# A hand-written order of 368 pieces replaced by another: memory-compressed attention followed by a maxout FFN on one core

## The chip, the cores and the metric

The kernel runs on one core of one Trainium2 chip. The metric is the device time of one execution in microseconds; lower is better. The kernel before takes 165.37 us (median of three runs, 165.14 to 165.49). TensorE is called PE, VectorE DVE, ScalarE ACT, GpSimd POOL and SyncE SP, as the profile does.

## The reference

Eight batches, eight heads, 576 positions, head size 64, 32 memory slots; then a feed-forward layer over 4608 rows of width 512 with a hidden width of 768.

```python
a = exp(phi - max(phi, axis=2)); a = a / sum(a, axis=2)       # softmax over positions
k_m = einsum('bhsm,bhsd->bhmd', a, k)                         # 32 slots instead of 576 keys
v_m = einsum('bhsm,bhsd->bhmd', a, v)
scores = q @ k_m.T / sqrt(64)
attn = softmax(scores)                                        # over the 32 slots
x = (attn @ v_m)  ->  rows (batch, position), columns (head, d)
h = maximum(maximum(x @ w1, x @ w2), x @ w3)
out = h @ w_out                                               # 4608 x 512, float32
```

## The kernel before, in words

All inputs are loaded with a cast to bf16 by POOL's DMA queue, except `phi`, which stays float32 (batch 0's `phi` comes through SP's queue). The 576 x 64 attention output is never formed. Because x = attn v_m, the kernel multiplies v_m into the weights for each batch ("fold") and applies the 32 slot weights to the folded weights. It also uses max(a, b, c) = max(a - c, b - c, 0) + c: w1 - w3 and w2 - w3 are formed in place, the relu of the first is a drain, the second is combined in a max, and the w3 part goes straight through `w3o` = w3 w_out into the output sum.

The work is cut into pieces, and one text, the word list at the end of the function, gives their order. A word is `letter+number@batch`; each piece issues its instructions on all engines at once, and every engine executes its own instructions strictly in the order of the list. So the list sets the order on PE, DVE, ACT, POOL and on the DMA queues. The letters, with the engine of the main work:

- `Y` weights, `L` and `H` inputs (k, v, q, phi; H loads half of the heads): DMA issues on POOL. `r`: POOL copies k or v into a packed tile (line 104).
- `E`: exp of phi on ACT (230). `B`: memory keys and values on PE (244). `N`: their normalisation on DVE (262 to 276). `K`: transposes of them on PE (291) and the drain of these (173 on ACT, 177 on DVE).
- `Q`: two transposes of q on DVE (306). `S`: scores on PE (326), then two exps on ACT (335). `a`, `s`, `c`: transpose, sum and reciprocal on DVE (380, 388, 397). `m`: slot softmax multiply on POOL (402). `X`: transpose back into `attn` on DVE (410). In batch 0 `M`, `R` and a DVE multiply (370) do this instead.
- `D0` to `D2`: folds of w1/w2 on PE (433) with a drain of 128x1024 from two PSUM banks into bf16 tile `wp`; `D3` the same for `w3o`. Batch 0 has `D4` too and shorter folds.
- `F0` to `F11`: first layer on PE (459). The even ones are drained with a relu (171 on ACT, 175 on DVE), the odd ones are combined with that on DVE by a max into `hT` (472).
- `T0` to `T4`: second layer on PE (490, 499, 508), drain into a float32 tile `ot` and a store on SP's queue. Odd batches have a fifth, `T4`, which spans two batches. The last, `T3@7`, is split in two (531 to 551).
- `W`, `O`: transposes of w3 and the product w3 w_out, once. `V`: the subtraction w - w3 on DVE (214). `Z`: matmuls on zeros at the start (160). `I`: constants.

PSUM has eight banks. Each piece takes the next digit of a second text, the bank list, as the number of its bank (a pair of banks for `B`, `S`, `D`, `F`, `M`; `S` takes two pairs). A bank's next piece waits until its drain is done.

Which engine drains a piece is read from a table, and a `!` behind a word exchanges ACT and DVE:

```python
EVAC = {"D": "avaaa", "T": "vavav", "K": "v", "W": "vvv", "O": "aaaa", "F": "aaaaaa"}
```

In the profile line 173 is ACT's copy (tiles `wp`, `ot`, `kvt`, `w3o`), line 177 DVE's, and matmul lines carry the tile `psum`.

Of the kernel before, what the change touches and what calls it, by code (L numbers as in the profile page):

```python
# [15 lines left out]
def kernel(  # L16
# [12 lines left out]
    nc = tc.nc  # L29

    B, H, S, D = q.shape
# [54 lines left out]
    def load_ph(b):  # L86
        ph = inp.tile([P, NP, NC, M], FP32, name="ph")
        loaded.setdefault(b, {})["ph"] = ph
        dst = ph.rearrange("p j c m -> p j (c m)")
        if b == 0:  # L90
            for h in halves:
                nc.sync.dma_start(out=dst[:, h], in_=by_pair(phi, b)[:, h])
        else:
            nc.gpsimd.dma_start(out=dst, in_=by_pair(phi, b))
# [8 lines left out]
    def pack(b, i):  # L103
        nc.gpsimd.tensor_copy(  # L104
            out=kvrs[b % 2][:, :, :, D * i : D * (i + 1)], in_=kvos[b % 2][:, i]
        )

    def load_q(b):
        qq = inp.tile([P, NP, NC, D], BF16, name="qq")
        loaded.setdefault(b, {})["q"] = qq  # L110
        nc.gpsimd.dma_start(  # L111
            out=qq.rearrange("p j c d -> p j (c d)"), in_=by_pair(q, b)
        )

    def load_w(i):
        w = (moe_w1, moe_w2, moe_w3)[i]
        nc.gpsimd.dma_start(
            out=w_sb[:, :, i], in_=w.rearrange("(j p) f -> p j f", p=P)
        )
# [3 lines left out]
    def load_wo():  # L123
        nc.gpsimd.dma_start(out=wo_sb, in_=moe_w_out.rearrange("(t p) c -> p t c", p=P))
# [8 lines left out]
    for i in range(P // M):  # L133
# [5 lines left out]
    banks = iter(  # L139
        "".join(  # L140
            """
            00224460026701101401264026402640264026452063420643064206420642064562074206742064
            20642064201640264102640264026402640264072406247026402640264024602406520462046204
            62704267402640264124602416420642064206420642067676767670
            """.split()
        )
    )
# [4 lines left out]
    def two_banks():  # L152
        i = int(next(banks))
        return psum[:, i : i + 2]
# [10 lines left out]
    EVAC = {"D": "avaaa", "T": "vavav", "K": "v", "W": "vvv", "O": "aaaa", "F": "aaaaaa"}  # L165

    def evacuate(kind, n, swap, out_, in_, relu=False):

        if (EVAC[kind][n] == "a") != swap:
            if relu:  # L170
                nc.scalar.activation(out=out_, in_=in_, func=AF.Relu)  # L171
            else:
                nc.scalar.copy(out=out_, in_=in_)  # L173
        elif relu:
            nc.vector.tensor_scalar_max(out=out_, in0=in_, scalar1=0.0)
        else:
            nc.vector.tensor_copy(out=out_, in_=in_)
# [28 lines left out]
    def columns(b, n):  # L206
        return FIRST[n] if b == 0 else (n * BANK, (n + 1) * BANK)
# [188 lines left out]
        s = st[b]  # L396
        nc.vector.reciprocal(out=s["sm", g], in_=s["sm", g])  # L397

    def att_mul(b, g):
        s = st[b]  # L400
        t = s["t", g]
        nc.gpsimd.tensor_tensor(  # L402
            out=t,
            in0=t,
            in1=s["sm", g].unsqueeze(2).to_broadcast([P, S // HP, R, 2]),
            op=ALU.mult,
        )
# [7 lines left out]
    wps, wp3s = {}, {}  # L415

    def fold(b, n, swap):

        s = st[b]
        lo, hi = (0, DM) if n == 3 else columns(b, n)  # L420
        if n == 3:
            wp3s[b] = quad.tile([P, NG, DM], BF16, name="wp3")
        elif b not in wps:
            wps[b] = work.tile([P, NG, 2 * DF], BF16, name="wp")
        ps = two_banks()
        terms = [(s["kvt"][:, 0], w3o[:, :, lo:hi] if n == 3 else w12[:, :, lo:hi])]
        if b == 0 and n != 3:
            terms.append((s["kvtn"], w_sb[:, :, 2, lo % DF : lo % DF + hi - lo]))
        for i, (lhs, rhs) in enumerate(terms):
            for j in range(NP):  # L430
                for a in range(NG):
                    r = slice(HP * a, HP * (a + 1))
                    nc.tensor.matmul(  # L433
                        ps[M * j : M * (j + 1), a, 0 : hi - lo],
                        lhsT=lhs[r, M * j : M * (j + 1)],
                        rhs=rhs[r, j, :],
                        start=(i == 0),
                        stop=(i == len(terms) - 1),
                        tile_position=(HP * a, M * j),
                    )  # L440
        evacuate(
            "D", n, swap, wp3s[b] if n == 3 else wps[b][:, :, lo:hi], ps[:, :, 0 : hi - lo]
        )


    hts = {}
# [107 lines left out]
    def issue(b, n, swap):  # L554

        i = int(n[1:]) if len(n) > 1 else None
        {
            "I": lambda: [make_identity(nc, ident)]
            + [nc.gpsimd.memset(x[:, :, :, 2 * D : 2 * D + 1], 1.0) for x in kvrs],
            "Y": lambda: load_w(i) if i < 3 else load_wo(),  # L560
            "L": lambda: load_ph(b) if i == 0 else load_q(b) if i == 3 else load_kv(b, i - 1),
            "H": lambda: load_kv(b, i % 2, halves[i // 2]),
            "r": lambda: pack(b, i),
            "E": lambda: [att_exp(b, h) for h in (halves if b == 0 else [slice(0, NP)])],
            "B": lambda: att_kv(b, i),
            "N": lambda: att_kv_norm(b, i),
            "K": lambda: att_kv_t(b, swap, i),
            "Q": lambda: att_q(b, i),
            "S": lambda: att_score(b),
            "a": lambda: att_t(b, i),  # L570
            "s": lambda: att_sum(b, i),
            "c": lambda: att_rec(b, i),
            "m": lambda: att_mul(b, i),
            "X": lambda: (ones_mul if (b, i) in ONES else att_back)(b, i),
            "M": lambda: ones_sum(b, i),
            "R": lambda: ones_rec(b, i),
            "D": lambda: fold(b, i, swap),
            "F": lambda: ffn1(b, i, swap),
            "T": lambda: ffn2(b, i, swap),
            "W": lambda: w3_t(i, swap),  # L580
            "O": lambda: w3_o(i, swap),
            "V": lambda: w_diff(i),
            "Z": lambda: warm_up(i),
        }[n[0]]()


    for w in """
        E@0 H2@0 H0@0 L3@0 Z25@0 B0@0 I@0 N0@0 Z2@0 K0@0! Q0@0 Q1@0 Z9@0 S@0 Z2@0 M0@0 M1@0
        R0@0 Y2@0 R1@0 W0@0 Y3@0 W1@0 W2@0 Z6@0 O1@0 H3@0 O3@0 O2@0 H1@0 X1@0 B1@0 X0@0 N1@0
        K1@0 O0@0 Y0@0 D1@0! D0@0! D3@0 F8@0 F10@0 F2@0 V0@0 F6@0 F0@0! Y1@0 D2@0 D4@0 F4@0  # L590
        L0@1 V1@0 F1@0 E@1 F3@0 L1@1 F5@0 F9@0 F7@0 L3@1 F11@0 B0@1 T3@0 N0@1 K0@1! L2@1 Q1@1
        L2@2 L1@2 Q0@1 L0@2 V2@0 T0@0! L3@2 S@1 T1@0 a0@1 s0@1 c0@1 m0@1 B1@1 N1@1 a1@1 L1@3
        K1@1 s1@1 D0@1 D1@1! D2@1 c1@1 m1@1 X0@1 L3@3 r1@2 X1@1 T2@0! L2@3 F6@1 F10@1 F7@1 F2@1
        F3@1 F4@1 F0@1 r0@2 E@2 F5@1 F1@1 F11@1 L0@3 L0@4 F8@1 L2@4 F9@1 B@2 D3@1 N@2 Q1@2
        T0@1! K@2 T2@1! r0@3 Q0@2 S@2 a0@2 a1@2 s1@2 c1@2 m1@2 T4@1! D1@2! s0@2 D2@2 c0@2 m0@2
        X1@2 D0@2 T3@1 Q0@3 L3@4 X0@2 Q1@3 T1@1 F0@2 F4@2 F8@2 F6@2 F9@2 E@3 F7@2 r1@3 F5@2
        F10@2 F1@2 B@3 L1@4 D3@2 N@3 L0@5 F2@2 F11@2 E@4 F3@2 L1@5 K@3 r1@4 L2@5 T2@2! S@3 T3@2
        a0@3 s0@3 c0@3 m0@3 D0@3 D2@3 a1@3 s1@3 c1@3 X0@3 D1@3! Q0@4 m1@3 T1@2 L3@5 L2@6 T0@2!
        X1@3 F10@3 r0@4 F2@3 F4@3 E@5 Q1@4 r0@5 F5@3 F3@3 L1@6 F8@3 B@4 N@4 D3@3 F9@3 F6@3
        F11@3 L0@6 K@4 F0@3 F7@3 F1@3 S@4 a0@4 T4@3! s0@4 a1@4 D0@4 c0@4 s1@4 r1@5 c1@4 D3@4  # L600
        m0@4 X0@4 Q0@5 T0@3! D1@4! D2@4 B@5 T3@3 m1@4 X1@4 L0@7 F10@4 Q1@5 N@5 F8@4 K@5 F6@4
        F9@4 S@5 F7@4 L3@6 F2@4 F4@4 a0@5 L1@7 a1@5 F0@4 s0@5 r1@6 F3@4 D0@5 r0@6 s1@5 c1@5 E@6
        D3@5 m1@5 c0@5 F1@4 T1@3 L2@7 F11@4 L3@7 E@7 F5@4 m0@5 B@6 D1@5! D2@5 X1@5 N@6 T2@3!
        X0@5 F6@5 F8@5 Q0@6 Q1@6 K@6 F4@5 F9@5 S@6 F7@5 r0@7 a0@6 F2@5 a1@6 s0@6 c0@6 F0@5
        F10@5 m0@6 F1@5 s1@6 c1@6 F11@5 F5@5 T0@4! F3@5 X0@6 T2@4! r1@7 D0@6 D1@6! Q0@7 B@7
        m1@6 N@7 X1@6 T2@5! K@7 T3@4 Q1@7 S@7 a0@7 F2@6 s0@7 a1@7 s1@7 c1@7 m1@7 c0@7 F4@6
        T4@5! D3@6 D2@7 D0@7! T0@5! D3@7 D2@6 X1@7 m0@7 D1@7! T1@4 X0@7 F6@7 F3@6 T1@5 F4@7
        F8@7 F0@7 F5@6 F10@6 F7@7 F9@7 F10@7 F5@7 F0@6 F11@7 F6@6 F1@7 F7@6 F2@7 F8@6 F11@6
        F9@6 F1@6 F3@7 T0@6! T0@7! T3@5 T2@7! T2@6! T1@6 T1@7 T3@6 T4@7! T3@7
    """.split():  # L610
        n, b = w.rstrip("!").split("@")
        issue(int(b), n, w.endswith("!"))


# [28 lines left out]
```

## Time and profile before

| | |
|---|---|
| median of three runs | 165.37 us |
| span of the profiled execution, first to last instruction | 163.1 us |
| the profiled execution's own time | no time of it is given beside its span; the median is 2.27 us longer than the span |
| PE busy | 152.5 us (93%), 2060 matmuls |
| ACT, DVE, POOL busy | 100.6, 94.3, 69.6 us |
| granted PE clock, mean | 0.997 |
| loaded and stored by DMA | 31.77 MB, mean 195 GB/s |

Line numbers (L459) are those of the kernel. In a group's row the count follows the x, then the busy time of the group and the mean length of one in ns. A matmul's length in a row includes the time in which it overlaps its neighbours; what one costs in a row of matmuls is read from the chain, where 48 in 5.88 us are 0.1225 us each. In the chain, each row is start, length, and the work that the end waited for.

### The profile page before, as it was taken

How to read it: one execution, taken by the hardware profiler on the slowest of the kernel's cores; microseconds unless marked ns; L12 is line 12 of the kernel's file. 1: busy time of each engine (PE TensorE's matmuls, PEld its weight loads, DVE VectorE, ACT ScalarE, POOL GpSimd, SP SyncE). 2: the span in 40 equal slices, each digit the busy share in tenths (PEclk: the TensorE clock that was granted, in tenths of full speed). 3: DMA queues.
4: the chain of work that ended last, by engine and by line, in shares of the span. 5: the costliest groups of instructions: out<-in, count | busy, mean ns of one | idle time of the engine just before them, and what ended most of it. 6: DMA issues, size and time to landing. Idle time of an engine off the chain costs nothing.

```text
span 163.1 us, 4818 instructions
## 1 busy us (share of the span) xinstructions
PE 152.5 (93%) x2060; PEld 85.2 (52%) x2080; DVE 94.3 (58%) x181; ACT 100.6 (62%) x151; POOL 69.6 (43%) x71
## 2 busy tenths in 40 slices
PE   7987798999899999999999999999999999999990
PEld 2443444664377436743673575576553467744440
DVE  6531704897838575848499758979749128800001
ACT  4206245926497488778876899994558976223320
POOL 7941205100699268647849966637403100000000
PEclk9999999999999999999999999999999999999998
DMA  5999999999999999999999999996323130024333
GB/s 155 153 205 209 207 210 215 274 208 208 262 308 237 209 255 375 277 209 296 249 263 207 235 348 267 191 237 147 129 80 119 68 129 0 0 77 183 129 135 125
DMA packets 21974, 31.77 MB, mean 195 GB/s; under 512 B 1216, under 2 KB 16576, under 8 KB 21952
## 3 DMA queue, kind: packets, MB, share of 16 engines
q0 software_dynamic: 16080, 21.43, 68.7%
q1 hardware_dynamic: 5728, 9.96, 17.3%
q8 instruction: 16, 0.26, 0.6%
q10 hardware_dynamic: 144, 0.07, 0.1%
q14 instruction: 6, 0.05, 0.1%
HBM read 39.32 MB, written 9.44 MB: 299 GB/s over the span
## 4 chain that ended last, share of the span: by engine, by line
PE 72%; DMA 20%; POOL 2%; issue 2%; DVE 1%; ACT 0%; POOLq 0%; ACTq 0%
PE psum L490 26%; PE psum L459 26%; DMA qq<-in_q_dram 13%; PE psum L499 8%; DMA w_sb<-in_moe_w_dram 7%; PE psum L433 4%; PE psum L244 3%; PE psum L326 2%; PE psum L508 1%; POOL kvo L98 1%; DVE qT L306 1%; PE psum L531 1%; PE psum L291 1%; POOL qq L111 0%; PE psum L539 0%
## 5 line engine op out<-in xcount | busy, mean ns | idle before, releaser
L490 PE MATMUL psum<-wo_sb,hT 128*128 128x512 bf16 x193 | 49.7, 380 | 1.3 <-issue 0.6
L459 PE MATMUL psum<-attn,wp 128*128 128x288 bf16 x384 | 50.5, 286 | 0.1
L472 DVE TENSOR_TENSOR hT<-psum,h 128x576 bf16<-128x576 f32 x48 | 34.2, 749 | 17.5 <-PE psum L459 12.0
L459 PEld LDWEIGHTS <-wp 128*128 128x128 bf16 x384 | 36.7, 98 | 13.2 <-issue 2.0
L173 ACT COPY ot<-psum 128x512 f32<-128x512 f32 x35 | 20.7, 591 | 32.1 <-PE psum L499 25.3
L490 PEld LDWEIGHTS <-hT 128*128 128x128 bf16 x210 | 19.2, 98 | 24.1 <-issue 4.3
L104 POOL COPY kvr<-kvo 128x2304 bf16<-128x2304 bf16 x12 | 25.4, 2115 | 14.4 <-DMA kvo<-in_k_dram 8.3
L173 ACT CAST wp<-psum 128x1024 bf16<-128x1024 f32 (+1 forms) x31 | 29.2, 996 | 3.3 <-PE psum L433 1.5
L171 ACT ACTIVATE h<-psum 128x576 bf16<-128x576 f32 x47 | 28.4, 659 | 3.4 <-PE psum L459 3.1
L402 POOL TENSOR_TENSOR t<-t,sm 128x576 bf16<-128x576 bf16 x14 | 16.1, 1156 | 24.3 <-DVE sm L397 24.2
L499 PE MATMUL psum<-wp,attn 128*128 128x512 bf16 x62 | 18.4, 379 | 0.0
L160 PE MATMUL psum<-warm 128*128 128x512 bf16 x42 | 11.9, 435 | 1.4 <-DVE warm L129 1.2
L306 DVE STREAM_TRANSPOSE qT<-qq 128x576 f32<-128x576 f32 x16 | 11.7, 747 | 1.9 <-DMA qq<-in_q_dram 1.9
L335 ACT ACTIVATE e<-psum 128x576 bf16<-128x576 f32 x16 | 9.6, 651 | 3.8 <-PE psum L326 3.8
L230 ACT ACTIVATE e<-ph 128x1152 bf16<-128x1152 f32 (+1 forms) x9 | 9.6, 1067 | 1.7 <-DMA ph<-in_phi_dram 1.6
L388 DVE TENSOR_REDUCE sm<-t 128x18 f32<-128x576 bf16 x14 | 10.3, 738 | 0.2
L98 POOL DMA_DIRECT2D kvo<-in_v_dram x9 | 6.7, 751 | 7.2 <-PE psum L244 4.1
L499 PEld LDWEIGHTS <-attn 128*128 128x128 bf16 x62 | 6.1, 98 | 7.1
L380 DVE STREAM_TRANSPOSE t<-e 128x288 f32<-128x288 f32 x14 | 6.4, 465 | 5.9 <-ACT e L335 5.8
L548 DVE COPY ot<-psum 128x384 f32<-128x384 f32 x1 | 0.6, 558 | 15.8 <-PE psum L539 15.8
L111 POOL DMA_DIRECT2D qq<-in_q_dram x8 | 6.2, 770 | 6.5 <-DMA w_sb<-in_moe_w_dram 6.5
L244 PEld LDWEIGHTS <-e 64*32 64x32 bf16 x720 | 6.9, 90 | 3.0 <-issue 2.6
(58 smaller groups left out, 118.0 us busy)
## 6 DMA issues: line engine op xcount, KB each, us to landing
out_dram<-ot SPq DMA_DIRECT2D x35, 256.0 KB, 5.5
qq<-in_q_dram POOLq DMA_DIRECT2D x8, 576.0 KB, 12.5
ph<-in_phi_dram POOLq DMA_DIRECT2D x7, 576.0 KB, 14.7
kvo<-in_k_dram POOLq DMA_DIRECT2D x7, 576.0 KB, 15.1
kvo<-in_v_dram POOLq DMA_DIRECT2D x7, 576.0 KB, 15.3
w_sb<-in_moe_w_dram POOLq DMA_DIRECT2D x3, 768.0 KB, 18.9
wo_sb<-in_moe_w_out_dram POOLq DMA_DIRECT2D x1, 768.0 KB, 14.6
ph<-in_phi_dram SPq DMA_DIRECT2D x2, 288.0 KB, 3.0
```

What stands on the lines that cost most here:

```text
L104: nc.gpsimd.tensor_copy(out=kvrs[b % 2][:, :, :, D * i : D * (i + 1)], in_=kvos[b % 2][:, i])
L160: nc.tensor.matmul(po[:, 0:BANK], lhsT=warm[:, 0:P], rhs=warm, start=True, stop=True)
L171: nc.scalar.activation(out=out_, in_=in_, func=AF.Relu)
L173: nc.scalar.copy(out=out_, in_=in_)
L244: nc.tensor.matmul(kvp[M * j : M * (j + 1), a, 0:nd], lhsT=s["e"][r, j, c, :], rhs=kv[r, cols, j, c, :] if b < FULL else kvr[r, j, c, 0:nd ...
L306: nc.vector.transpose(out=s["qT"][:, j].rearrange("p j c r e -> p (j c r e)").bitcast(FP32), in_=loaded[b]["q"][:, j].rearrange("p j c d - ...
L388: nc.vector.tensor_reduce(out=sm, in_=s["t", g].rearrange("p n r e -> p n e r"), op=ALU.add, axis=mybir.AxisListType.X,)
L402: nc.gpsimd.tensor_tensor(out=t, in0=t, in1=s["sm", g].unsqueeze(2).to_broadcast([P, S // HP, R, 2]), op=ALU.mult,)
L459: nc.tensor.matmul(acc[:, h, 0:SH], lhsT=wps[b][:, g, w * DF + ft * P : w * DF + (ft + 1) * P], rhs=attn[:, g, c0 : c0 + SH], start=(g == ...
L472: nc.vector.tensor_tensor(out=hT[:, ft, (b % 2) * S : (b % 2 + 1) * S].rearrange("p (h n) -> p h n", h=2), in0=a, in1=s["h1", ft], op=ALU.max,
L490: nc.tensor.matmul(po, lhsT=hT[:, fc, c0 : c0 + P], rhs=wo_sb[:, fc, :], start=(n == 0), stop=False,)
L499: nc.tensor.matmul(po, lhsT=attn[:, g, c0 : c0 + P], rhs=wp3s[b][:, g, :], start=False, stop=(g == NG - 1),)
```

## The change

Five things change; the pieces are the same 368, and so are the arithmetic and the bytes.

1. The word list has a new order, and the bank list is new (216 digits each).
2. The head of POOL's DMA queue is w3, k (two halves), q, w_out, v (two halves), w1, w2; before it was k (two halves), q, w3, w_out, v (two halves), w1, w2. After w2 both go on with phi, k, q, v of batch 1, and then v, k, phi, q of batch 2.
3. `!` may stand on `m`: the multiply then runs on DVE in place of POOL. Six of the fourteen carry it (m1@1, m0@2, m1@2, m1@3, m0@5, m1@7).
4. A new mark `*` on a fold: its drain is halved, 128x512 on ACT and 128x512 on DVE. Eleven of the 33 folds carry it.
5. Other drains exchange engines. Counted over the list, before to after: `T` on DVE 0 to 13 (of 36 whole ones), even `F` on DVE 1 to 12 (of 48), whole folds on ACT 31 to 21 and on DVE 2 to 1, `K` on ACT 2 to 8 (of 10), `W` on ACT 0 to 2 (of 3), `O` on DVE 0 to 1 (of 4).

```diff
-        if (EVAC[kind][n] == "a") != swap:
+        if (EVAC[kind][n] == "a") != (swap == "!"):
...
-    def att_mul(b, g):
+    def att_mul(b, g, swap):
...
-        nc.gpsimd.tensor_tensor(
+        (nc.vector if swap else nc.gpsimd).tensor_tensor(
...
-        evacuate(
-            "D", n, swap, wp3s[b] if n == 3 else wps[b][:, :, lo:hi], ps[:, :, 0 : hi - lo]
-        )
+        to = wp3s[b] if n == 3 else wps[b][:, :, lo:hi]
+        if swap == "*":
+            nc.scalar.copy(out=to[:, 0], in_=ps[:, 0, 0 : hi - lo])
+            nc.vector.tensor_copy(out=to[:, 1], in_=ps[:, 1, 0 : hi - lo])
+        else:
+            evacuate("D", n, swap, to, ps[:, :, 0 : hi - lo])
...
-            "m": lambda: att_mul(b, i),
+            "m": lambda: att_mul(b, i, swap == "!"),
...
-        E@0 H2@0 H0@0 L3@0 Z25@0 B0@0 I@0 N0@0 Z2@0 K0@0! Q0@0 Q1@0 Z9@0 S@0 Z2@0 M0@0 M1@0
-        R0@0 Y2@0 R1@0 W0@0 Y3@0 W1@0 W2@0 Z6@0 O1@0 H3@0 O3@0 O2@0 H1@0 X1@0 B1@0 X0@0 N1@0
-        K1@0 O0@0 Y0@0 D1@0! D0@0! D3@0 F8@0 F10@0 F2@0 V0@0 F6@0 F0@0! Y1@0 D2@0 D4@0 F4@0
-        L0@1 V1@0 F1@0 E@1 F3@0 L1@1 F5@0 F9@0 F7@0 L3@1 F11@0 B0@1 T3@0 N0@1 K0@1! L2@1 Q1@1
-        L2@2 L1@2 Q0@1 L0@2 V2@0 T0@0! L3@2 S@1 T1@0 a0@1 s0@1 c0@1 m0@1 B1@1 N1@1 a1@1 L1@3
-        K1@1 s1@1 D0@1 D1@1! D2@1 c1@1 m1@1 X0@1 L3@3 r1@2 X1@1 T2@0! L2@3 F6@1 F10@1 F7@1 F2@1
...
+        E@0 Y2@0 H0@0 Z9@0 Z25@0 H2@0 Z2@0 B0@0 I@0 N0@0 Z6@0 L3@0 Y3@0 W1@0! H1@0 W0@0! Q0@0
+        Q1@0 H3@0 W2@0 K0@0! S@0 M0@0 M1@0 R1@0 Y0@0 Z2@0 O3@0! X1@0 O2@0 B1@0 N1@0 R0@0 X0@0
+        Y1@0 O0@0 K1@0 O1@0 L0@1 D1@0! D0@0 D3@0 F8@0! F10@0! F6@0 L1@1 V0@0 F4@0 L3@1 F2@0
+        D2@0! D4@0 V2@0 F0@0 F3@0 E@1 F1@0 L2@1 F5@0 F9@0 F7@0 F11@0 B0@1 N0@1 Q0@1 T3@0 Q1@1
+        K0@1! L2@2 L1@2 T2@0! V1@0 S@1 a0@1 T0@0! B1@1 a1@1 s0@1 L0@2 N1@1 K1@1 L3@2 L0@3 c0@1
+        L1@3 D1@1! D0@1 s1@1 L2@3 L3@3 D2@1 c1@1 m1@1! m0@1 r1@2 L2@4 X0@1 r0@2 X1@1 r0@3 r1@3
+        T1@0 F0@1! F6@1 F7@1 F8@1 F4@1 F1@1 F2@1 E@2 F9@1 F10@1 F5@1 F3@1 F11@1 L1@4 B@2 D3@1
+        L0@4 N@2 Q0@2 T0@1! K@2! Q1@2 L3@4 T4@1 r1@4 S@2 a0@2 s0@2 L1@5 a1@2 s1@2 c0@2 T3@1!
+        D0@2 c1@2 D1@2! m0@2! X0@2 D3@2* m1@2! T1@1 E@3 X1@2 T2@1 D2@2 B@3 F8@2 L2@5 N@3 F6@2
...
+        D1@4* m1@4 D2@4* B@5 D3@4 c0@4 N@5 Q0@5 D0@4 Q1@5 m0@4 T2@3! X1@4 K@5! T4@3! S@5 X0@4
+        F10@4! a0@5 a1@5 F6@4 L3@6 s1@5 F2@4 F4@4 F8@4 F3@4 F9@4 F5@4 c1@5 s0@5 F0@4 r0@6 c0@5
+        L1@7 F11@4 r1@6 F7@4 F1@4 L0@7 m0@5! m1@5 r1@7 E@6 L3@7 T0@3! D1@5* B@6 X0@5 D0@5* X1@5
+        D2@5 T1@4 N@6 F0@5! F8@5 F9@5 F2@5! F10@5 r0@7 F6@5 F4@5 E@7 F7@5 K@6! F11@5 F1@5 F5@5
...
+        F5@7 F0@6 F1@6 T0@7! F3@6 T2@7! T1@7 F5@6 T2@6! T0@6 T4@7 T1@6! T3@6! T3@7
     """.split():
-        n, b = w.rstrip("!").split("@")
-        issue(int(b), n, w.endswith("!"))
+        n, b = w.rstrip("!*").split("@")
+        issue(int(b), n, w[-1])
```

More of the change, by code (lines that the diff above doesn't have):

```diff
@@ L141 @@
             """
-            00224460026701101401264026402640264026452063420643064206420642064562074206742064
-            20642064201640264102640264026402640264072406247026402640264024602406520462046204
-            62704267402640264124602416420642064206420642067676767670
+            01020103246046764760640264204624062406267046474602640246240264206736020643246024
+            02640620467420670246064264026426046201264026726402640264026042604240260420462050
+            26412460520636042340624062046024062460246204647647676767
             """.split()
@@ L594 @@
[L594 to L609, printed above, removed]
+        E@0 Y2@0 H0@0 Z9@0 Z25@0 H2@0 Z2@0 B0@0 I@0 N0@0 Z6@0 L3@0 Y3@0 W1@0! H1@0 W0@0! Q0@0
+        Q1@0 H3@0 W2@0 K0@0! S@0 M0@0 M1@0 R1@0 Y0@0 Z2@0 O3@0! X1@0 O2@0 B1@0 N1@0 R0@0 X0@0
@@ new lines @@
+        D0@2 c1@2 D1@2! m0@2! X0@2 D3@2* m1@2! T1@1 E@3 X1@2 T2@1 D2@2 B@3 F8@2 L2@5 N@3 F6@2
+        F2@2 F7@2 Q1@3 F3@2 F10@2 F9@2 F4@2 F11@2 F5@2 F0@2 F1@2 Q0@3 L0@5 r0@4 K@3! T2@2 L3@5
+        S@3 a1@3 a0@3 D3@3 s0@3 s1@3 T3@2 c0@3 E@4 T0@2! c1@3 m1@3! X1@3 m0@3 D0@3* X0@3 D2@3
+        L2@6 B@4 D1@3! N@4 T1@2! Q0@4 F10@3 r0@5 Q1@4 F0@3 F6@3 r1@5 F11@3 F1@3 F7@3 F4@3 F2@3
+        F5@3 L1@6 F3@3 K@4! F8@3 F9@3 S@4 a0@4 L0@6 a1@4 L2@7 s1@4 c1@4 T3@3 E@5 s0@4 T1@3!
+        D1@4* m1@4 D2@4* B@5 D3@4 c0@4 N@5 Q0@5 D0@4 Q1@5 m0@4 T2@3! X1@4 K@5! T4@3! S@5 X0@4
@@ new lines @@
+        F10@4! a0@5 a1@5 F6@4 L3@6 s1@5 F2@4 F4@4 F8@4 F3@4 F9@4 F5@4 c1@5 s0@5 F0@4 r0@6 c0@5
+        L1@7 F11@4 r1@6 F7@4 F1@4 L0@7 m0@5! m1@5 r1@7 E@6 L3@7 T0@3! D1@5* B@6 X0@5 D0@5* X1@5
+        D2@5 T1@4 N@6 F0@5! F8@5 F9@5 F2@5! F10@5 r0@7 F6@5 F4@5 E@7 F7@5 K@6! F11@5 F1@5 F5@5
+        Q0@6 T2@4! D1@6* Q1@6 D3@5* B@7 Q1@7 D2@6* N@7 T3@4 F3@5 T0@4 S@6 K@7! Q0@7 a0@6 T2@5!
+        a1@6 s1@6 c1@6 s0@6 c0@6 S@7 T1@5 a1@7 s1@7 m1@6 c1@7 m0@6 a0@7 D0@7 D3@6* D3@7 X0@6
+        m1@7! X1@6 T0@5 T4@5! s0@7 c0@7 D2@7 D1@7* m0@7 D0@6 X1@7 X0@7 T3@5! F6@7! F10@6 F8@7!
@@ L610 @@
+        F7@7 F0@7 F11@6 F1@7 F6@6 F9@7 F8@6! F2@6! F2@7 F10@7! F7@6 F4@7! F9@6 F4@6 F3@7 F11@7
+        F5@7 F0@6 F1@6 T0@7! F3@6 T2@7! T1@7 F5@6 T2@6! T0@6 T4@7 T1@6! T3@6! T3@7
     """.split():
-        n, b = w.rstrip("!").split("@")
-        issue(int(b), n, w.endswith("!"))
+        n, b = w.rstrip("!*").split("@")
+        issue(int(b), n, w[-1])
 _INS = ['q', 'k', 'v', 'phi', 'moe_w1', 'moe_w2', 'moe_w3', 'moe_w_out']
```

## The prediction

> **What bounds the kernel now.** I read the page's slices first, then the chain of waits, the waits of each engine, and last the groups for prices.
>
> ```profile
> PE   7987798999899999999999999999999999999990
> DVE  6531704897838575848499758979749128800001
> ACT  4206245926497488778876899994558976223320
> DMA  5999999999999999999999999996323130024333
> ```
>
> PE is full from about 24 us to 160; until 110 us the DMA engines are full too. The chain (start, length, what the end waited for) says which of the two decides when:
>
> ```profile
> 4.26 11.50 DMA w_sb<-in_moe_w_dram
> ...
> 16.05 21.61 DMA qq<-in_q_dram
> ...
> 37.69 1.45 DVE qT L306 x2
> ...
> 39.18 0.48 PE psum L326 x23
> ...
> 45.83 5.88 PE psum L459 x48
> ...
> 58.20 0.55 PE psum L508 x4
> 58.76 0.77 PE psum L433 x24
> 59.53 1.40 PE psum L490 x6
> 60.93 0.43 PE psum L499 x2
> 61.36 1.29 PE psum L490 x6
> 62.66 0.43 PE psum L499 x2
> ```
>
> Up to 39.18 (S@1) the end hangs on landings: w3 at 15.76, batch 1's q at 37.67. Behind that nearly every piece of the chain is a matmul. A row of `F` costs 5.88/48 = 0.1225 us a matmul, 0.49 a piece; a `T` costs 1.29 + 0.43 = 1.72; a fold 0.77/3 = 0.26. The `T` behind folds takes 1.40 instead of 1.29: 0.11 us for the change from 64x32 tiles to the full array. PE's own waits from 45 to 160 us, and its busy time from 45.83 on:
>
> ```profile
> PE psum L490 <- issue: 0.6, 4, 0.2
> 45.83:159.36 113.53, 112.27 (x1436) 64.70 (x1448) 67.95 (x134) 78.80 (x118) 52.37 (x43) 1.00 0.79 192
> ```
>
> By the prices above (and 0.73 for `B`, 0.40 for `S`, 0.17 for `K`) the pieces from F6@1 to the end are 110.9 us of matmuls; they took 113.5. The 2.6 us between hold 18 runs of tiled pieces (`B`, `S`, `D`) at 0.11 to 0.14 each, and nothing else of size. So behind 46 us this order loses nothing to drains or to PSUM. A new order can gain there only by fewer changes of tile shape; it can lose wherever a drain comes late.
>
> **The sum's own time.** The profiled span is 163.1 us; the runs have a median of 165.37. I take the 2.27 us outside the span as unchanged. About 0.2% (0.33 us) is what a measurement here can tell from no change.
>
> **The head, to D1@0.** Both orders have the same PE pieces ahead of D1@0 and the same bytes ahead of w1 on POOL's queue. In the trace the casting loads follow each other without a gap: k's halves land at 7.25 and 8.65, q 11.55, w3 15.76, w_out 19.6, v 22.4, w1 26.1, w2 30.0. D1@0 began at 26.26, 0.2 us of it a wait for w1. With w3 first (it took 4.2 us, q 2.9, a half of k 1.4), w3 lands at about 10, k at 11.0 and 12.4, q at 15.3 to 15.8; w_out, v, w1 stay. B@0 falls from 8.81 to about 12.5; the nine warm-up matmuls moved ahead of it end at about 11, so PE idles 1.5 us. S@0 falls from 12.7 to about 17.3 (q landed, two transposes of 0.73). The w3 transposes then fill what was waiting time. From w_out at 19.6 on, O3, O2, B1, O0, K1 and O1 are four times 1.29, 0.73 and 0.06: 5.95 us, ending at 25.6 to 25.9, just under w1's 26.1. DVE's X1, N1, X0 and the drain of K1 lie in there, the last at about 25.3. So the head costs 0, with -0.5 (w3's larger packets) to +0.7 (that cover of 0.2 us gone) as bounds. Ahead of q of batch 1, the order of loads is the same again. In before, each issue on POOL from the eleventh on waits for the landing eight places earlier (k of batch 1 for q, q of batch 1 for w3, v of batch 1 for w_out); afterwards q of batch 1 waits for q of batch 0, at the same 15.8. So S@1 stays pinned near 39.2.
>
> **D1@0 to F of batch 1.** Before, DVE did one fold drain (1.23), two subtractions (1.22 and 1.28), one relu (0.76) and six maxes (4.07) from 27.18 on and ended at 36.18. T3@0 waited on the last `hT` and lost under 0.1 us. Afterwards it has two relus (F8, F10: 1.5), two subtractions (2.4), D2's drain (0.6 to 0.7) and the six maxes, 8.7 us, but cannot begin before F8 is out at about 28.1: end 36.8. T3@0 then waits 0.5, of which the wait for q hides a part: +0.3. Behind S@1, batch 1's softmax on DVE is 4.5 us of listed work before and 5.2 afterwards (m1@1 comes to DVE). m0@1 on POOL moves behind two issues (v and q of batch 3, 0.76 each) that wait for B1@1 at 42.2, so it ends at 45.0. X1@1 ends near 46.0 instead of 45.8: +0.2.
>
> **Moves between the engines.** The prices:
>
> ```profile
> L402 POOL TENSOR_TENSOR t<-t,sm 128x576 bf16<-128x576 bf16 x14 | 16.1, 1156 | 24.3 <-DVE sm L397 24.2
> ...
> L370 DVE TENSOR_TENSOR attn<-e,r 128x576 bf16<-128x576 bf16 x2 | 1.4, 750 | 0.0
> L175 DVE TENSOR_SCALAR h<-psum 128x576 bf16<-128x576 f32 x1 | 0.8, 758 | 0.7 <-ACT h L171 0.7
> ```
>
> DVE's broadcast multiply isn't in the trace. The nearest row is L370, the same size from two SBUF operands: 0.73; bounds 0.42 (the transposes over the same tile) and 1.16 (POOL's own). A 128x512 drain on DVE lies between 0.56 (128x384) and 1.23 (128x1024): 0.69; on ACT it is 0.59. DVE gains 13 `T` (9.0), 11 relus (8.3), 11 half folds (7.6), 6 multiplies (4.4) and an `O` (0.7), and gives up 6 `K`, 2 `W` and a fold (4.5): 94.3 + 25.5 = about 120 us, 73% of the span. ACT falls to about 87, POOL by 6 x 1.156 to 62.7. Relief of ACT and POOL is worth nothing here: no PE wait behind 46 us names either. The load on DVE counts where PE waits for it, and that is between S and the first F of a batch, where both `X` must be done. From the lists, PE work / DVE work (us) in that stretch, batches 1 to 7:
>
> before 5.0/4.5, 6.1/4.6, 5.9/4.6, 7.0/4.6, 9.1/8.7, 12.6/9.4, 7.8/5.1;
> after 5.0/5.2, 6.9/6.7, 6.9/5.3, 9.3/8.5, 10.8/11.7, 11.3/8.0, 8.5/7.6.
>
> DVE begins about 0.8 after S (39.66 to 40.44 in batch 1), and work back to back is some 7% shorter than its rows (six maxes of 0.749 took 4.07). PE's side is 3 to 5% longer by changes of tile shape. Batch 5 is then short by 11.7 - 11.2 = 0.5 us, batch 2 by up to 0.2, batch 1 by the 0.2 above; the others are covered. PSUM is reused sooner too: pieces that find less than a microsecond of matmuls between a bank's last writer and themselves are 14 before and 34 afterwards, most at 0.98, where a relu or max (0.65 to 0.76) needs its engine free at once. Cost 0 to 1 us; I take 0.2.
>
> **Fewer changes of shape.** From D1@0 on the list has 24 runs of tiled pieces, afterwards 21: -3 x 0.126 = -0.4.
>
> **The tail** stays: T3@7 last and split, its bank free 1.4 us or more ahead, stores behind it.
>
> **Sum.** 0 (head) + 0.3 + 0.2 (batch 1) + 0.5 + 0.1 (batches 5 and 2) + 0.2 (PSUM) - 0.4 = +0.9 us. In batch 5 folds are halved, so that both halves are out some 0.3 us sooner than one drain of 0.94 on ACT; I take that off the 0.5 and keep +0.6: span 163.7, time 166.0.
>
> **Rivals.**
> 1. *The order holds* (chance 0.25): all joins are met, as the long stretches K to S and S to F of batches 2 to 5 would have it, and only the shape changes are left, with a head up to 0.4 better: -0.2 to -0.8, about 164.9. For it: ACT is at 9 tenths of 92 to 108 us before, and is relieved. Against it: PE shows no wait there that this could take away.
> 2. *DVE and POOL exclude each other* (0.20): a multiply on DVE that reads two SBUF tiles waits while POOL reads SBUF. The trace of before can't show it: its POOL copies lie within 2099 to 2147 ns, its POOL multiplies within 1148 to 1179, but no DVE operation with two SBUF operands runs beside them. Afterwards m1@1 stands beside m0@1 on POOL, m0@2 and m1@2 beside copies of 2.1 us, m1@3, m0@5 and m1@7 beside POOL work. Half a POOL operation (0.6 to 1.05) for six multiplies is 3.5 to 6.3 us of DVE; with joins as tight as above about 2 reach PE: 167.9 with the forecast's 0.6. It decides once two of the joins are met later than 0.5 us. The Trainium skill ("SBUF — State Buffer", section "Who interferes with whom") says that a VectorE instruction with two SBUF inputs contends with a GpSimd instruction that reads SBUF, the second waiting for the first; no run here shows it yet.
> 3. *Nothing net* (0.10): stalls of some 0.4 us cancel the shape changes: 165.4.
>
> The forecast itself, DVE late at a few joins, has 0.45.
>
> **Chances and range.** Slower by over 0.2%: 0.40 of the forecast's 0.45 and rival 2's 0.20, 0.60. Same: 0.05 of the forecast, 0.04 of rival 1, rival 3: 0.19. Faster: 0.21. The range runs from rival 1 with its head (164.5) to rival 2 (168.0); the forecast's own is 165.4 to 167.0.
>
> **What would show it.** DVE busy near 115 to 120 us, POOL near 63. D1@0 at 26.0 to 27.0; S@1 at 39.2 to 39.7; the first F of batch 1 at 46.0 to 46.6. Waits of PE on DVE's `attn` or `hT`, in the stretch of batch 5 above all. POOL copies or DVE multiplies longer than 2.15 and 0.8 us would be rival 2. The forecast is wrong if S@1 comes before 38.5 (a faster head), or if PE's gaps behind 46 us stay at 2.3 us (rival 1).

## The result, and the profile after

The change makes the kernel slower: 173.93 us (173.29 to 174.04, four runs) against 165.38 for before on the same chip, a ratio of 1.051 (95% interval 1.049 to 1.053). The span is 172.2 us, 9.1 longer. The forecast was 166.0 within 164.5 to 168.0: the sign was right, the size far off, and the time lies outside the range.

The page's slices of the changed kernel, with the granted PE clock, which was 9 throughout before:

```profile
PE   7987499999749999799999999999999999999991
DVE  6403332898893869979799895997999989961231
ACT  4201628944554647563976787666637674322100
PEclk9999879999996999999999999999999999999998
DMA  5999999999999999999999999989032231004333
```

PE has holes in slices 5, 12 and 17, and the clock drops behind the first two. The chain of waits (start, length, what the end waited for) goes through other things than before:

```profile
2.87 10.84 DMA kvo<-in_k_dram
...
17.31 1.02 ACT w3T L173
18.33 0.29 ACT kvt L173
...
18.66 0.59 PE psum L326 x25
...
46.91 3.63 DVE t L402
50.54 0.40 DVE attn L410
50.98 7.78 PE psum L462 x48
```

Ahead of S@0 (18.66) stand k and two drains of w3T (the transposed w3) on ACT. At 46.91 a DVE multiply takes 3.63 us, and the 48 `F` matmuls behind it take 7.78 us where they took 5.88. Four moments of PE give the account:

| us | D1@0 | S@1 | first F of batch 1 | last matmul ends |
|---|---|---|---|---|
| before | 26.26 | 39.18 | 45.66 | 159.28 |
| changed | 28.95 | 41.89 | 50.98 | 168.35 |
| lost in the stretch | 2.7 | 0.0 | 2.6 | 3.8 |

The last stretch takes 117.4 us instead of 113.6. Of its 3.8 us, 1.9 are those 48 matmuls. The rest goes with the multiply m0@2: in e2 below, where it meets no POOL copy, the stretch takes 115.5 us, the slow 48 matmuls included.

The windows (PE, PEld, DVE, ACT, POOL busy, clock, DMA share, GB/s) show both falls of the clock; 0.50 is half speed:

```profile
18.00:20.00 2.00, 0.55 (x33) 0.36 (x34) 0.60 (x2) 1.37 (x4) 0.00 (x0) 1.00 1.19 199
20.00:22.00 2.00, 1.64 (x6) 0.83 (x7) 0.00 (x0) 1.28 (x3) 0.74 (x1) 0.64 1.20 208
22.00:24.00 2.00, 2.00 (x6) 0.75 (x5) 0.00 (x0) 0.48 (x1) 0.00 (x0) 0.51 1.16 211
...
48.00:50.00 2.00, 0.52 (x3) 0.12 (x2) 2.00 (x1) 1.67 (x3) 1.92 (x1) 1.00 1.17 283
50.00:52.00 2.00, 1.02 (x5) 0.59 (x5) 1.29 (x3) 0.00 (x0) 1.79 (x2) 0.82 1.13 300
52.00:54.00 2.00, 2.00 (x10) 1.24 (x9) 0.76 (x1) 0.65 (x1) 1.13 (x1) 0.50 1.14 285
54.00:56.00 2.00, 2.00 (x15) 1.47 (x14) 0.90 (x2) 1.13 (x2) 0.00 (x0) 0.83 1.18 233
```

Each fall follows a stretch in which PE was busy for about a quarter of the time. The groups put the price on the multiplies, and the timeline around the first shows what it waited for:

```profile
L402 DVE TENSOR_TENSOR t<-t,sm 128x576 bf16<-128x576 bf16 x6 | 10.4, 1736 | 0.1
```
```profile
46.70 1.18 POOL L402 TENSOR_TENSOR t<-t,sm 128x576 bf16<-128x576 bf16 x1
46.91 3.63 DVE L402 TENSOR_TENSOR t<-t,sm 128x576 bf16<-128x576 bf16 x1
47.80 2.11 POOL L104 COPY kvr<-kvo 128x2304 bf16<-128x2304 bf16 x1
```

POOL's copy ends at 49.91; the multiply ends 0.63 later, at 50.54. The same 0.6 behind the end of a POOL multiply or copy stands at m0@2 (2.50 us), m1@3 (1.69) and m0@5 (1.14). The two with nothing of that kind beside them take 0.74 and 0.72.

Times below are medians over all runs of a kernel; the ratios to before on the same chip, and the intervals in brackets, leave out runs that are more than 1.5% above the fastest of their kernel, as kernels that leave PE idle in places spread more than before does (e1 had a mean clock of 1.000 in two runs and 0.980 in the other two).

### The profile page after: what moved, and what is told of

Its sections match the earlier page's. It is cut to its first block, busy times and chain, and to the rows that moved or that the text cites. A ratio compares the mean times of both kernels' runs of the same rounds, so it can differ in the third digit from the quotient of the medians.

```text
span 172.2 us, 4837 instructions
## 1 busy us (share of the span) xinstructions
PE 156.9 (91%) x2059; PEld 87.7 (51%) x2080; DVE 121.5 (71%) x214; ACT 88.5 (51%) x135; POOL 62.6 (36%) x65
## 4 chain that ended last, share of the span: by engine, by line
PE 70%; DVE 15%; DMA 6%; issue 3%; ACT 3%; POOL 1%; ACTq 0%; DVEq 0%; POOLq 0%
PE psum L462 27%; PE psum L493 20%; DMA kvo<-in_k_dram 6%; PE psum L502 6%; DVE t L402 6%; PE psum L193 4%; PE psum L244 3%; PE psum L433 3%; DVE hT L475 2%; PE psum L326 2%; DVE sm L388 2%; DVE wp L444 1%; PE psum L511 1%; DVE attn L410 1%; PE psum L160 1%
## 5 line engine op out<-in xcount | busy, mean ns | idle before, releaser
L462 PE MATMUL psum<-attn,wp 128*128 128x288 bf16 x384 | 51.6, 292 | 2.7 <-DVE attn L410 2.5
L462 PEld LDWEIGHTS <-wp 128*128 128x128 bf16 x384 | 37.7, 99 | 16.4 <-issue 4.3
L171 ACT ACTIVATE h<-psum 128x576 bf16<-128x576 f32 x36 | 22.3, 655 | 18.8 <-PE psum L462 18.6
L173 ACT COPY ot<-psum 128x512 f32<-128x512 f32 x22 | 12.9, 588 | 21.6 <-PE psum L502 18.3
L173 ACT CAST wp<-psum 128x1024 bf16<-128x1024 f32 (+1 forms) x21 | 20.3, 1003 | 5.8 <-PE psum L433 5.7
L402 POOL TENSOR_TENSOR t<-t,sm 128x576 bf16<-128x576 bf16 x8 | 9.2, 1156 | 31.4 <-DVE sm L397 29.8
L177 DVE COPY ot<-psum 128x512 f32<-128x512 f32 x13 | 8.8, 680 | 8.6 <-PE psum L502 5.9
L175 DVE TENSOR_SCALAR h<-psum 128x576 bf16<-128x576 f32 x12 | 8.8, 751 | 5.2 <-PE psum L462 5.2
L402 DVE TENSOR_TENSOR t<-t,sm 128x576 bf16<-128x576 bf16 x6 | 10.4, 1736 | 0.1
L433 PE MATMUL psum<-w_sb,kvt 64*32 64x512 bf16 (+1 forms) x200 | 8.9, 373 | 1.5 <-DVE wp L444 1.2
## 6 DMA issues: line engine op xcount, KB each, us to landing
kvo<-in_k_dram POOLq DMA_DIRECT2D x7, 576.0 KB, 11.3
```

The source lines that it names most:

```text
L402: (nc.vector if swap else nc.gpsimd).tensor_tensor(out=t, in0=t, in1=s["sm", g].unsqueeze(2).to_broadcast([P, S // HP, R, 2]), op=ALU.mult,)
L433: nc.tensor.matmul(ps[M * j : M * (j + 1), a, 0 : hi - lo], lhsT=lhs[r, M * j : M * (j + 1)], rhs=rhs[r, j, :], start=(i == 0), stop=(i == ...
L462: nc.tensor.matmul(acc[:, h, 0:SH], lhsT=wps[b][:, g, w * DF + ft * P : w * DF + (ft + 1) * P], rhs=attn[:, g, c0 : c0 + SH], start=(g == ...
```

## Experiments 1 to 4: the multiplies and the head

**e1, POOL writes but doesn't read.**

```diff
-        nc.gpsimd.tensor_copy(
-            out=kvrs[b % 2][:, :, :, D * i : D * (i + 1)], in_=kvos[b % 2][:, i]
-        )
+        nc.gpsimd.memset(kvrs[b % 2][:, :, :, D * i : D * (i + 1)], 0.01)
```

> The changed kernel with the twelve POOL copies that pack k and v (r) replaced by POOL memsets of the same regions: batches 2 to 7 use a constant for k and v, so this part of the computation is left out, and POOL writes SBUF there but doesn't read it. Theory A (a DVE multiply with two SBUF operands waits until a POOL instruction that reads SBUF ends): the first multiply, 3.63 us in the changed kernel, ends at the end of POOL's own multiply, some 1.6 to 1.7 us long; m0@2, 2.50 us, falls to 0.72; m1@3 beside POOL's multiply stays at 1.7. The first F of batch 1 moves from 50.98 to about 49.0 and the median from 173.9 to 169 to 171. Rival B (the multiply is slow whenever POOL is busy, writing too): multiplies of 2 us and more stay and the time stays above 172.5. Rival C (the multiply is slow by itself or DVE is overloaded): multiplies and time as in the changed kernel.

168.78 us, 1.023 (1.016 to 1.030). Two places of its timeline:

```profile
45.52 1.18 POOL L400 TENSOR_TENSOR t<-t,sm 128x576 bf16<-128x576 bf16 x1
45.73 1.59 DVE L400 TENSOR_TENSOR t<-t,sm 128x576 bf16<-128x576 bf16 x1
...
105.03 2.01 POOL L104 MEMSET kvr<- 128x2304 bf16 x1
106.61 0.75 DVE L400 TENSOR_TENSOR t<-t,sm 128x576 bf16<-128x576 bf16 x1
```

The first multiply now ends 0.6 behind POOL's multiply and no longer waits for the pack. The one beside a memset isn't delayed at all. Theory A holds; B and C fall. (The first F of batch 1 came at 47.8, sooner than the 49.0 expected, and the median just under the range.) The Trainium skill ("SBUF — State Buffer", "Who interferes with whom") says just this: two SBUF inputs on VectorE contend with a GpSimd instruction that reads SBUF, not with one that only writes. The trace agrees, 1.59 to 3.63 us against 0.75. The packs here don't wait for landings either, so the gain of 5 us isn't the price of the multiplies' waits alone.

**e2, the head of before.** Words and banks ahead of D1@0 as in before, the rest as changed.

```diff
-        E@0 Y2@0 H0@0 Z9@0 Z25@0 H2@0 Z2@0 B0@0 I@0 N0@0 Z6@0 L3@0 Y3@0 W1@0! ...
+        E@0 H2@0 H0@0 L3@0 Z25@0 B0@0 I@0 N0@0 Z2@0 K0@0! Q0@0 Q1@0 Z9@0 S@0 ...
```

> The changed kernel with the order, marks and banks of before for all pieces ahead of D1@0 (w3 behind k and q again), and everything from D1@0 on as changed. Theory H (the head alone lost 2.7 us, and it is carried to the end unchanged): D1@0 back at 26.3, clock 1.0 from 20 to 24 us, median 171.2 (170.7 to 171.7). Rival (what follows takes the gain back, since S@1 waits for batch 1's q at 37.7 and the multiply ends with POOL's copies): 172.5 to 174.

169.90 us, 1.029 (1.022 to 1.037): 4 us gained, more than the 2.7 expected; the rival is out. D1@0 is at 26.53, S@1 at 40.23. The multiply of batch 1 is the same (3.63 us, and the half clock behind it), but m0@2 no longer meets a copy (0.69 us in place of 2.50). That copy, r1@4, waits for v of batch 4 to land. In the changed kernel it started 0.2 us ahead of the multiply, here 1.2 us behind its end. What a DVE multiply costs thus depends on when a transfer lets POOL's copy go.

**e3, before with the six multiplies on DVE.**

```diff
-        ... c1@1 m1@1 X0@1 ...
+        ... c1@1 m1@1! X0@1 ...
```

(and so for m0@2, m1@2, m1@3, m0@5, m1@7)

> The kernel before with nothing changed but the six multiplies m1@1, m0@2, m1@2, m1@3, m0@5, m1@7 on DVE. Theory A (only what POOL reads at that moment matters): in this order POOL's copies stand elsewhere in batches 1 and 2 (r1@2 behind m1@1, r1@3 behind the multiplies), so multiplies are 0.7 us, and up to 1.7 beside a POOL multiply or a copy; 165.0 to 166.5. Rival C (a DVE multiply is slow by itself, 1.7 us on average): each of six costs a microsecond on DVE and the time is 167 or more.

Both expectations miss: the four runs lie between 170.2 and 180.1 us, too far apart for a ratio, and all are above before (165.0). The timeline of the run at 180.1 us shows why the "0.7, up to 1.7" of theory A was too low:

```profile
82.56 0.75 POOL L98 DMA_DIRECT2D kvo<-in_v_dram  x1
82.90 6.53 DVE L402 TENSOR_TENSOR t<-t,sm 128x576 bf16<-128x576 bf16 x1
83.29 4.17 POOL L104 COPY kvr<-kvo 128x2304 bf16<-128x2304 bf16 x2
...
87.39 0.74 POOL L98 DMA_DIRECT2D kvo<-in_k_dram  x1
88.13 0.76 POOL L94 DMA_DIRECT2D ph<-in_phi_dram  x1
88.88 2.52 POOL L104 COPY kvr<-kvo 128x2304 bf16<-128x2304 bf16 x1
90.00 2.32 PE L462 MATMUL psum<-attn,wp 128*128 128x288 bf16 x9 [5.39 <-DVE attn L410]
```

The multiply isn't served between two POOL copies; it ends 0.55 behind the start of the third, which in turn takes 2.52 us instead of 2.11. PE waits 5.39 us for `attn`, 11.3 us in four such waits over the run. One part of the change alone costs 5 to 15 us in the old order. m1@1 takes 3.41 us there too: it begins beside POOL's issue of q's load, 0.66 ahead of the copy r1@2, and ends 0.63 behind that copy.

**e4, warm-ups in the head.**

```diff
-        ... K0@0! S@0 M0@0 ...
+        ... K0@0! Z6@0 S@0 Z3@0 M0@0 ...
```

> The changed kernel with six warm-up matmuls more behind K0@0 and three more behind S@0, where PE waits (17.4 to 18.7 and 19.1 to 19.9 us). Theory K (the clock fell to half from about 20.5 to 24 because PE was little used before it): granted clock 1.0 from 20 to 24, the O pieces take 0.215 a matmul, D1@0 at 27.5 to 28.0 in place of 28.95 and the median 172.5 to 173.0. Rival (the clock falls for another reason, or the O pieces wait for v anyway): no change, 173.9.

172.55 us, 1.040 (1.033 to 1.048). The windows that answer to those above:

```profile
20.00:22.00 2.00, 1.83 (x11) 0.90 (x10) 0.00 (x0) 1.48 (x4) 0.74 (x1) 1.00 1.20 207
22.00:24.00 2.00, 2.00 (x10) 0.75 (x8) 1.11 (x2) 0.45 (x1) 0.00 (x0) 1.00 1.17 211
```

Matmuls on zeros keep the clock at 1.00, and D1@0 moves from 28.95 to 27.43. Of the head's 2.7 us, 1.5 were the clock, and the median came out as theory K said. The Trainium skill ("TensorE: Matmul & The Clock Gate", Part 1) states half clock after an idle window of some 3.4 us and full clock after a busy one, with windows that run freely. The changed kernel's trace agrees on the length of a fall (20.6 to 24.0 us and 51.3 to 54.7, so 3.4 each), but not on idle: PE was busy for 0.55 and 0.52 of the 2 us shown ahead of the two falls. e1's run at 167.1 us kept the clock with the same head and 0.49 of the same 2 us busy.

## Experiments 5 to 8: undoing in pairs, and single parts in before

**e5 and e6, all multiplies on POOL**, with the old and with the new head.

```diff
-        ... c1@1 m1@1! m0@1 r1@2 L2@4 X0@1 r0@2 X1@1 r0@3 r1@3 T1@0 ... r1@4 S@2 a0@2 s0@2 L1@5 ...
+        ... c1@1 m0@1 m1@1 r1@2 L2@4 X0@1 r0@2 X1@1 T1@0 ... S@2 a0@2 s0@2 ...
-        ... m0@2! X0@2 D3@2* m1@2! T1@1 ...
+        ... m0@2 X0@2 D3@2* m1@2 r0@3 r1@3 r1@4 L1@5 T1@1 ...
```

> The changed kernel with two parts undone: the head of before, and all multiplies on POOL again (m0@1 ahead of m1@1; the copies r0@3, r1@3, r1@4 and the load L1@5 moved behind the multiplies of batch 2, so that these don't wait for landings). Left of the change are the order from D1@0 on, the banks, the halved folds and the exchanged drains. Theory A+H (multiplies beside POOL and the head are the whole loss): no PE wait for attn longer than 0.5 us, clock 1.0 throughout, 164.5 to 166. Rival O (the new order and the DVE load cost something of their own): 167 or more, with DVE late at other pieces.

> As the last one, but with the new head: only the multiplies (and the copies behind them) are undone. Theory A+H: the head is left, D1@0 at 27.5 to 29, so 1.5 to 2.7 us above the last one, 166.5 to 168.5. Rival: later pieces absorb the head, within 0.5 us of the last one.

171.88 us, 1.041 (1.036 to 1.046), and 173.64 us, 1.053 (1.047 to 1.058): both are far above what A+H expected. The waits of PE in e5 name my own edit:

```profile
PE psum L244 <- POOL kvr L104: 3.4, 1, 3.4
PE psum L462 <- DVE attn L410: 0.7, 1, 0.7
```

B@3 waits 3.4 us for the copies that I had put behind the multiplies, and the clock is at half from 67 to 74 us. So these two say nothing on the order itself. They suggest that in this order POOL's time in batch 2 is needed for the packs; the multiplies of batch 2 back on POOL with the packs left where they were wasn't tried. Their difference, 1.8 us, agrees with the 1.5 to 2.7 expected for the head.

**e7, before with the new head.**

```diff
-        E@0 H2@0 H0@0 L3@0 Z25@0 B0@0 I@0 N0@0 ...
+        E@0 Y2@0 H0@0 Z9@0 Z25@0 H2@0 Z2@0 B0@0 ...
```

> The kernel before with only the new head: all pieces up to D1@0 in the new order with the new marks and banks, the rest as before. Theory H (the head delays D1@0 by 1.5 to 2.7 us and everything behind it is PE without gaps): 166.5 to 168. Rival (S@1 is pinned by batch 1's q, which lands as before, so that the delay is absorbed ahead of it): 165.0 to 165.6.

166.84 us, 1.011 (1.005 to 1.017). D1@0 at 29.3, S@1 at 42.0, the last matmul ends 2.9 later than in before. Theory H holds: the head is carried to the end whole. The single times are 167.8 and 167.4 where the mean clock was 0.990 and 0.985, 166.3 and 166.0 where it was 1.00.

**e8, before with the new drains** (all marks of the changed list but those on `m`).

```diff
-        ... T0@1! K@2 T2@1! ...
+        ... T0@1! K@2! T2@1 ...
```

> The kernel before with all marks of the changed list but those on m: eleven halved folds, and T, F, K, W, O drains on the engines of the changed kernel; order, banks and multiplies as before. DVE gets some 21 us more. Theory (drains on DVE cost only where PE waits for them): 165 to 166.2. Rival O (the DVE load is a cost of its own, waits for hT and attn): 167 or more.

175.04 us, 1.058 (1.053 to 1.064). Rival O holds in this order, and strongly. Behind 45 us PE has seven kinds of wait, all of them for DVE; the three longest are:

```profile
PE psum L326 <- DVE qT L306: 1.5, 1, 1.5
PE psum L291 <- DVE kvn L266: 1.5, 1, 1.5
PE psum L462 <- DVE h L175: 1.3, 1, 1.3
```

DVE works in the order of the list, so a `T` or a relu on it stands ahead of the transposes of q, the normalisation or the next relu. In the new order the same drains stand in e9 below, at 167.26 us; so what a drain on DVE costs is a matter of the order.

## Experiments 9 to 12: what is left

**e9, old head and m1@1 on POOL**; the other five stay on DVE, and no pack moves.

```diff
-        ... c1@1 m1@1! m0@1 r1@2 ...
+        ... c1@1 m0@1 m1@1 r1@2 ...
```

> The changed kernel with the head of before and one multiply moved: m1@1 back on POOL, behind m0@1. The other five multiplies stay on DVE and no copy is moved. Theory A+H (two places made the loss, the head and the multiply beside POOL's copy in batch 1 with the half clock behind it; the rest of the change is worth about nothing): first F of batch 1 at 46 to 46.6 instead of 49.3 with the old head alone, clock 1.0 from 48 to 56, median 165.0 to 166.0. Rival O (the order, the banks and the DVE load cost on their own): 167 or more.

167.26 us, 1.012 (1.008 to 1.016). The first F of batch 1 stands at 46.2 (0.7 us of wait for the second `attn` half inside it), and the clock is 1.00 from 48 to 56. Two edits take 1.051 to 1.012. A+H is right on the two places but misses the time, and rival O's 167 is met, just: 1.2% stays. In its trace m0@5 meets a copy (1.86 us), and F0@5 behind it waits 0.17 for `attn` and 0.46 behind a drain and N@6.

**e10, before with w3 first.**

```diff
-        E@0 H2@0 H0@0 ... R0@0 Y2@0 R1@0 ...
+        E@0 Y2@0 H2@0 H0@0 ... R0@0 R1@0 ...
```

> The kernel before with one word moved: the load of w3 goes to the front of POOL's queue, ahead of k; nothing else changes. Theory H1 (the head is lost because k and then S@0 come 5 us later, so that PE has less to do before w_out and falls to half clock): k complete at 13.7, S@0 at 17 to 18, D1@0 at 27.5 to 29, 166.3 to 168. Rival H2 (the new order of the pieces ahead of D1@0 is to blame, w3 first is hidden): D1@0 within 0.4 of 26.3 and the time as before.

169.20 us, 1.024 (1.019 to 1.030). B@0 begins at 14.5, S@0 at 20.5, D1@0 at 31.8. From the windows:

```profile
10.00:14.00 4.00, 0.00 (x0) 0.00 (x0) 0.00 (x0) 0.00 (x0) 1.50 (x2) 0.92 1.21 207
14.00:20.00 6.00, 5.15 (x83) 2.46 (x85) 2.22 (x5) 0.37 (x1) 1.48 (x2) 0.50 1.23 208
```

H2 falls. H1 is right on the way but too low in all its figures: PE stands idle from 10 to 14 us, the clock is at half from 13.4 to 20.2, and w3 first alone costs more than the whole new head in e7. So the new order of the pieces (nine warm-ups forward, `W` ahead of `S`) makes good a part of it.

**e11, e9 with everything ahead of S@1 as in before and m1@3 on POOL.**

```diff
-        ... F8@0! F10@0! F6@0 ... T2@0! V1@0 S@1 a0@1 T0@0! ...
+        ... F8@0 F10@0 F2@0 ... T0@0! L3@2 S@1 a0@1 T2@0! ...
-        ... c0@3 E@4 T0@2! c1@3 m1@3! X1@3 m0@3 D0@3* X0@3 ...
+        ... c0@3 m0@3 E@4 T0@2! c1@3 m1@3 X0@3 X1@3 D0@3* ...
```

> As the first of this call, and two more parts undone: all pieces ahead of S@1 stand as in before (T0@0 there, T2@0 behind S@1), and m1@3 goes to POOL, behind m0@3. Theory A+H: S@1 at 39.2, first F of batch 1 at 45.8 to 46.2, no multiply on DVE longer than 1.2 us; with three runs of tiled pieces fewer in the list 164.4 to 165.2, level with before or just under it. Rival O: 166.5 or more.

166.88 us, 1.011 (1.006 to 1.016), in rival O's range. S@1 is at 39.0 as in before, the first F of batch 1 at 45.5, and yet 1.1% stays. All of it lies behind that F: from there to the last matmul e11 takes 115.5 us and before 113.6. Its PE waits on DVE from 46 us on:

```profile
PE psum L462 <- DVE attn L410: 0.7, 1, 0.7
...
PE psum L462 <- DVE kvn L276: 0.3, 1, 0.3
```

and its chain runs through DVE between S and the first F of batches 2, 3 and 5, and through POOL's multiplies in batch 1. The two waits are 1.0 of the 1.9 us; PE's busy time from 46 us on is 0.7 longer too (112.8 against 112.1). No version tried beats before.

**e12, e7 with the warm-ups of e4.** The edit is that of e4.

> The kernel before with the new head (all pieces up to D1@0) and, in it, six warm-up matmuls more behind K0@0 and three behind S@0, where PE waits. Theory K (half of the new head's cost, or more, is the half clock from 20.5 to 24): clock 1.0 from 18 to 28, D1@0 at 27.4 to 27.9 instead of 29.3, and a median some 1.5 us under that of the new head without them, 165.3 to 166.3. Rival (the loss is w3 ahead of k and the drains of w3T ahead of kvt's, and the clock hides in it): D1@0 at 28.8 or later, 166.5 or more.

167.22 us over eleven runs (165.43 to 168.10), 1.008 (1.005 to 1.012); e7 had 1.011 (1.005 to 1.017). The profile bears theory K out, clock 1.00 from 12 to 28 and D1@0 at 27.8 in place of 29.3. The times don't: the median is above the range expected, the intervals overlap, and in four of the runs the mean clock was 0.985 to 0.988 all the same. So nine warm-up matmuls don't hold the clock in every execution, and 1.5 us are left in D1@0 with the clock kept.

## Why the prediction was wrong, by its own steps

Two terms of the sum failed most: the head (0, measured 2.7) and the join of batch 1 (0.2, measured 2.6, with 1.9 of half clock behind it). The sum held nothing for the clock, and nothing for a DVE multiply's wait on POOL, which stood among the rivals only.

- **The head, "0, with -0.5 to +0.7".** Measured +2.7, the first step that failed, in three parts. The landings came about 1 us later than read: k was complete at 13.7 instead of 12.4, q at 16.6 instead of 15.3 to 15.8, and w_out, which was to stay at 19.6, at 20.7. Behind them S@0 came at 18.66, not 17.3: q's transposes ended at 18.0, and kvt's drain 0.6 after that, because on ACT two w3T drains of some 1.0 us stood ahead of it, an exchange of engines that I had listed and priced but not followed in ACT's order. (This is read from the trace; no run moves these drains alone.) O3 then began at 21.7, a microsecond behind w_out. And the sum had no clock in it: 12 matmuls of `O` took 3.86 us instead of 2.6, and with the clock kept D1@0 came 1.5 us sooner (e4).
- **S@1 "pinned near 39.2".** It came at 41.89. Between D1@0 and S@1 nothing was absorbed: q of batch 1 landed at 38.05, DVE came to it at 39.80, and PE had no gap left ahead of S@1. Even with the old head the new order has S@1 at 40.23 (e2) and 39.62 (e9).
- **m1@1 and "+0.2" at batch 1.** The stretch S@1 to F took 9.1 us instead of 6.5. Nothing but the wait of the multiply is in it: with m1@1 on POOL behind m0@1 (e9, e11) it took 6.6 in both, with 0.7 us of wait inside F.
- **Rival 2** had the mechanism, with chance 0.20 and a price of 2 us. Shown by e1: reading counts, writing doesn't. Too small were two things: half a POOL operation for each, where m1@1 waited for a multiply and a whole copy in a row (3.63), and the step from a PE wait to the clock, which made 2.5 us of wait cost another 1.9 (7.78 against 5.88 for 48 matmuls).
- **The forecast's own case, "DVE late at a few joins", +0.6.** What e9 and e11 leave, 1.1 to 1.2% or 1.8 to 2.0 us, is in part of this kind: e11's chain goes through the joins that were named (batches 1, 2 and 5) and through batch 3, but the waits that name DVE add up to 1.0 us only. The prices of single operations held: a `T` drain on DVE 0.68 (0.69 expected), the free multiply 0.69 to 0.76 (0.73), DVE 121.5 us busy (about 120), POOL 62.6 (62.7), ACT 88.5 (87).
- **"-0.4" for three runs of tiled pieces fewer** didn't show. In e11 PE's busy time from 46 us on is 0.7 longer than in before, and the 144 matmuls of the w1/w2 folds in it take 6.8 us instead of 5.6. Why they do, and how much each late join of e11 costs, wasn't settled; nor were the bank list and the halved folds undone by themselves.

## What to carry to other kernels

When an instruction with two SBUF operands is moved from POOL to DVE, look at what POOL reads at that moment: what matters is the longest row of POOL instructions that can stand in front of it, not its own length. A piece that is exchanged between engines has to be followed in the order of both, the small drain behind it above all. And where PE is close to always busy, price a hole of two microseconds with the half clock that may follow it.

## What the runs showed of the hardware

A DVE multiply of two SBUF tiles takes 0.69 to 0.76 us alone. Held up by a POOL multiply or copy, or by one of each in a row, it ends 0.60 to 0.66 us after the last one's end; in a row of two POOL copies and two DMA issues it took 6.53 us (e3). The wait goes the other way too: a POOL copy that began 0.15 us behind a multiply that nothing held up took 2.56 us instead of 2.11 and ended 1.97 behind it (e2); the same 1.97 stands behind m1@2 in the changed kernel and behind the 6.53 us multiply in e3. Whether POOL's DMA issues hold the multiply off is open: in e3 two multiplies weren't served beside them (m1@1 and the one of 6.53 us), while m1@2 ran beside one in 0.74 us in the changed kernel, in e9 and in e11. DVE transposes and reductions ran inside POOL's copies at their usual length (0.83 for two transposes in before, 0.75 for a reduction in e9).

The PE clock fell to half after stretches of two microseconds and more with PE a quarter busy or idle. It stayed there for some 3.4 us in the changed kernel and for some 6.8 us in e5 and e10. In the new head it fell in some executions and not in others.
